# Tap rows as four products summed in PSUM, one shared exponential buffer and a new instruction order in an S4 convolution kernel

## The chip, the cores and the metric

The kernel runs on one core of a Trainium2 chip. The metric is the device time of one launch in microseconds (us), as the median of several runs. Some runs of a kernel take longer than the others: a run more than 1.5% above the fastest of the same kernel is called slow here, and all ratios use fast runs only. The granted clock is the share of full TensorE speed that the profile records; its mean does not tell slow from fast in this case (0.927 in the slow run of the changed kernel, 0.897 to 0.941 in its fast ones). Within a trace, TensorE is called warm where the granted clock is 1.00 and cold where it is 0.50. The traces have a span that starts at the first and ends at the last instruction; it is about 1.8 us shorter than the device time of the same run. Times "at" are us from the start of that span.

## The reference, cut to what matters

The output is a gated mix of a long convolution (S4) and a small routed feed-forward network. Only the first matters for the change.

```python
# L = 2048 steps, D = 512 channels, N = 128 modes
logdA = dt * (A_re + 1j * A_im)                      # D x N
P = jnp.exp(logdA[:, :, None] * l[None, None, :])    # l = 0 .. L-1
K = jnp.einsum("dn,dnl,dn->dl", Cc, P, dt * Bc).real # convolution kernel, D x L
y = irfft(rfft(u, 2 * L) * rfft(K, 2 * L))[:L] + u * Dskip
out = g * y + (1 - g) * routed_ffn(u)                # g: a sigmoid gate per step
```

The kernel does not compute all L exponentials of a mode. It writes a lag as a sum of an entry of a first table (32 lags) and an entry of a second (21 "slots"), makes both tables as exponential times sine or cosine, and lets TensorE contract their product over the modes. The transforms are matmuls with fixed matrices.

## The kernel before: the parts that matter

The channels are worked on in two halves of 256, h = 0 and 1. The rows of the second table (the "tap rows") hold 21 slots. Slots 0 to 8 come from exponentials and sines; slots 9 to 20 are complex products of earlier slots with two base values, made on VectorE. A complex product takes six operations: four multiplications, and two that combine.

```python
def cmul(h, outs, a, b, rda, rdb, wr):          # VectorE; index 0 imaginary, 1 real
    TT(q(0), a(0), b(0), MUL, ...)
    TT(q(1), a(1), b(0), MUL, ...)
    TT(outs(1), a(1), b(1), MUL, ...)
    TT(outs(0), a(0), b(1), MUL, ...)
    TT(outs(1), outs(1), q(0), SUB, ...)        # combine
    TT(outs(0), outs(0), q(1), ADD, ...)        # combine
# at the end of tab2(h):
cmul(h, ... slots 13 to 20 = slots 0 to 7 times base 1 ...)   # 128 x 2048 each
cmul(h, ... slots 9 to 12 = slots 5 to 8 times base 0 ...)    # 128 x 1024 each
```

The product of the two tables, `kgen`, follows on TensorE. I call it the tap-row product. It has 256 matmuls per half, each with 64 columns of weights and 42 moving columns. They add up in PSUM, TensorE's output memory; an eviction is the copy of a finished PSUM buffer by another engine:

```python
def kgen(h):
    for b0 in range(0, 64, 12):                  # 12 groups of 4 channels fill one PSUM buffer
        ...
        for g in range(b0, b0 + ng):
            for ct in range(2):
                for part in range(2):
                    hh.matmul(pb(64 * ct, 64, (g - b0) * 42, (1, 42)), TP[h][1 - part](...),
                              TQ[h][1 - part](0, 128, g * 84 + ct, (2, 42)),
                              start=(part == 0), stop=(part == 1), tile_position=(0, 64 * ct))
        EV(KA[h](...), pb(...), ...)             # eviction, on ScalarE or VectorE
    ...
```

After it come the spectrum of the convolution kernel (TensorE), the products of the spectra (VectorE, with some sums made by accumulating DMAs issued by GpSimd), the inverse transform (TensorE) and the output. Three more facts matter:

- The order of all some 620 operations is a fixed list `SEQ`; each engine works through its own part strictly in that order. A negative entry puts an operation that ScalarE or VectorE can do on VectorE.
- The 2 MB of inverse matrices, `G` (in the trace `c_inv`), are loaded to where first-table values of the second half lie, so their load starts when the last matmul of the second tap-row product is done.
- The input with the routed part added is read back from memory (`xp`, 2 MB, the "reload") for the output.

Of the kernel before, what the change touches and what calls it, by code (L numbers as in the profile page):

```python
# [9 lines left out]
BF = mybir.dt.bfloat16  # L10
# [48 lines left out]
class Prog:  # L59
# [48 lines left out]
    def schedule(self):  # L108
# [7 lines left out]
        for n in SEQ:  # L116
# [21 lines left out]
            if o.dma:  # L138
                t0 = st + (0.8 if e == POOL else c + 1.2)
                if o.nbytes > 20000:  # L140
                    t0 = max(t0, dma_free[e])
                took = o.nbytes / (150.0e3 if o.tag == "sum" else self.DMA_BW)
                if e != SP and dma_free[SP] > t0:
                    w = min(dma_free[SP] - t0, 7.0)
                    dma_free[SP] += took
                    if o.nbytes > 20000:
                        t0 += w
                    took *= 1.3
                if o.nbytes > 20000:
                    dma_free[e] = t0 + took  # L150
                o.end = t0 + took + 0.5 + o.late
            else:
                o.end = st + c + (0.13 if e == PE else 0.0)
# [130 lines left out]
def kspec_mats():  # L284
# [35 lines left out]
    "0 19 3 2 1 4 8 22 23 54 57 41 55 40 49 50 64 24 25 58 59 56 63 42 26 27 -179 -169 -167 -168 -180 -170 43 -177 39 37 5 -207 211 -178 170 -172 -174 180 "  # L320
    "-182 -184 184 17 172 -187 -189 182 -199 -188 68 9 210 -213 78 46 47 45 12 6 208 207 -210 213 66 217 65 84 -200 11 51 75 52 -190 10 29 28 30 31 32 103 "
    "185 48 36 91 77 53 18 20 21 61 -198 67 80 44 71 73 216 218 83 90 214 -216 38 86 72 60 107 62 15 112 -114 -115 -116 -121 121 14 223 222 16 122 123 85 "
    "174 175 76 70 13 219 220 124 125 126 127 144 128 -225 229 228 74 190 -194 -192 194 196 200 -204 -202 204 221 225 226 129 130 132 -132 133 134 135 192 "
    "195 256 258 259 136 7 -232 230 236 137 257 260 -262 263 138 139 140 202 -269 -266 -267 -268 205 141 142 162 145 34 227 233 232 -144 262 264 275 -317 "
    "276 274 269 -271 272 163 277 280 281 278 279 -314 282 283 164 271 273 284 285 -304 305 286 89 150 151 315 104 235 93 105 35 111 87 154 -156 79 33 152 "
    "156 98 237 242 241 362 96 -307 110 109 81 234 239 314 108 238 361 95 99 243 248 102 -305 287 289 -154 106 69 82 94 288 292 299 291 290 298 293 294 88 "
    "240 244 245 101 97 100 92 157 158 159 295 297 301 247 296 300 345 317 -321 318 319 -334 334 336 335 321 322 343 307 308 309 323 325 324 326 -311 311 "
    "312 337 -341 -339 341 346 349 -351 160 344 347 -349 327 -331 331 246 251 353 339 342 -381 -382 379 378 328 329 -372 -370 -371 -373 351 367 352 365 366 "
    "368 250 363 -253 354 355 357 -357 359 249 332 382 -384 385 373 374 375 389 388 376 -388 390 393 -392 394 384 254 358 253 364 377 386 392 395 398 397 "
    "399 396 400 402 401 405 406 404 412 403 407 409 411 408 413 255 410 414 360 419 420 415 421 452 416 451 453 417 418 423 422 455 427 431 432 424 425 "  # L330
    "454 456 428 429 430 433 434 146 147 -149 -150 161 165 435 436 426 437 438 116 117 118 119 439 441 -443 440 443 465 464 466 461 444 445 446 447 448 462 "
    "463 449 450 488 484 483 489 500 490 471 472 457 458 460 459 502 504 473 474 478 485 546 486 501 505 477 547 548 503 467 468 469 470 487 492 549 491 "
    "496 497 550 557 551 493 556 558 475 302 506 507 508 509 510 498 499 560 494 495 559 561 513 515 514 516 518 517 511 512 519 522 476 524 526 525 527 "
    "479 480 482 481 531 532 533 538 540 539 528 529 535 536 537 541 523 530 534 567 520 552 553 555 581 579 554 578 580 562 563 565 564 582 589 583 590 "
    "584 591 592 594 593 595 585 587 586 588 521 566 568 569 544 573 543 571 603 601 545 542 598 599 570 602 600 597 596 572 574 575 576 577 610 612 611 "
    "613 615 619 614 618 604 606 605 607 608 616 609 617 "
).split()]

KB = 1024


def bass_gated_mix__ssm_conv_s4__moe_arch_mod__prompt_kernel(nc, A_u, A_A_re, A_A_im, A_B_re, A_B_im, A_C_re, A_C_im, A_log_dt, A_Dskip,
# [22 lines left out]
    with ExitStack() as es:  # L365
# [63 lines left out]
        o_ = [190 * KB]  # L429
# [4 lines left out]
        CB = small("cb", 1792, BF); CF = small("cf", 640, F32); AL = small("al", 2048, F32); B16 = small("b16", 2048, F32)  # L434
        WW = small("ww", 2048, BF); SG = small("sg", 256, F32); SGB = small("sgb", 128, BF); RTS = small("rts", 1088, F32)
        OHT = small("oht", 64, BF); ZB = small("zb", 1024, BF); WL = small("wl", 16, BF); XS = small("xs", 16, BF)
        HB = small("hb", 448, BF); MSB = small("msb", 16, BF); DSK = small("dsk", 1024, BF); EB1 = small("eb1", NM * 512, BF); IDX = small("idx", 32, I32); HPI = small("hpi", 32, F32)
        assert o_[0] <= SBW, o_[0]
        oA, oB, oC, oD, oE, oF, oG, oI = [x * KB for x in (0, 16, 48, 64, 96, 117, 149, 170)]
# [16 lines left out]
        EB = [B("eb0", oG, NM * 512), EB1]  # L456
        XP = Buf(P, "xp", AR[:, :], "dram", 0, 4, BF)
        xp = nc.dram_tensor("xp", (L, D), BF).ap()
        QA = [B("qa%d" % i, o, 9 * KB) for i, o in enumerate((oG + NM * 512, oE))]
        BN = [(B("bni%d" % i, o, KB), B("bnr%d" % i, o + KB, KB)) for i, o in enumerate((oG + 14 * KB, oE + 9 * KB))]  # L460
        UN = B("un", oG + 16 * KB, 4 * KB)
# [3 lines left out]
        KA = [B("ka0", oG, 64 * 84), B("ka1", oE, 64 * 84)]  # L465
# [6 lines left out]
        SL = [B("sl%d" % i, o, 4 * KB) for i, o in enumerate([oI + 4 * KB * k for k in range(4)] + [oD + 26 * KB, oE + 11 * KB, oE + 15 * KB] + [oG + 4 * KB * k for k in range(1, 5)] + [oD + (6 + 4 * k) * KB for k in range(4)])]  # L472
        PR = [[(SL[4], SL[5], SL[6], SL[0]), tuple(SL[7:11])], [(SL[0], SL[1], SL[11], SL[12]), (SL[2], SL[3], SL[13], SL[14])]]
        YA = [B("ya%d" % i, o, 4 * KB) for i, o in enumerate((oI + 16 * KB, oE))]
# [81 lines left out]
        def two(buf, other, off, st):  # L556

            a, c = buf(0, 128, off, (st, 64), (1, 4)), other(0, 128, off, (st, 64), (1, 4))
            return bass.AP(a.tensor, a.offset, [a.ap[0], [c.offset - a.offset, 2], [st, 64], [1, 4]])
# [3 lines left out]
        def exps2(ts):  # L563
            for b in EB:
                P.op(POOL, lambda h, b=b: h.memset(b(0, 128, 0, (4 * NM, 64), (1, 4)), 1.0), [], [(b, ("e", 0))], cost=0.4)
            for i, m in enumerate(MAG2):
                if i:
                    AC(two(EB[0], EB[1], i * 4, 4 * NM), AL(0, 128, 0, (HC, 2), (4, 64), (1, 4)), ACTF.Exp, [AL], [(EB[0], ("e", i)), (EB[1], ("e", i))], scale=float(m), tset=ts)
# [48 lines left out]
        def tab2(h, ts):  # L617
            (qi, qr), (bi, br), eb = TQ[h], BN[h], EB[h]
# [19 lines left out]
            bn = lambda p, j, c: (bi, br)[p](0, 128, 4 * j, (8, 64), (0, c), (1, 4))  # L638
            cmul(h, lambda p: sl(p, 13, 8), lambda p: sl(p, 0, 8), lambda p: bn(p, 1, 8), ks, [bi, br], lambda p: [(tq(p), "n")])
            cmul(h, lambda p: sl(p, 9, 4), lambda p: sl(p, 5, 4), lambda p: bn(p, 0, 4), ks, [bi, br], lambda p: [(tq(p), "f")])  # L640
# [141 lines left out]
        def kgen(h):  # L782
            for b0 in range(0, 64, 12):
                ng = min(12, 64 - b0)
                pb = kgp[(b0 // 12) % 2]
                def mm(hh, b0=b0, ng=ng, pb=pb):
                    last = None
                    for g in range(b0, b0 + ng):
                        for ct in range(2):
                            for part in range(2):  # L790
                                last = hh.matmul(pb(64 * ct, 64, (g - b0) * 42, (1, 42)), TP[h][1 - part](0, 128, g * 128 + ct, (2, 64)),  # L791
                                                 TQ[h][1 - part](0, 128, g * 84 + ct, (2, 42)), start=(part == 0), stop=(part == 1), tile_position=(0, 64 * ct))
                    return last
                P.op(PE, mm, [*TP[h], *TQ[h]], [pb.buf], cost=ng * 4 * 0.03)
                EV(KA[h](0, 128, b0 * 42, (1, ng * 42)), pb(0, 128, 0, (1, ng * 42)), [pb.buf], [(KA[h], b0)])
# [82 lines left out]
        def inverse(h):  # L878
            for blk in (1, 0):
# [35 lines left out]
                for st in range(4):  # L915
                    tb = blk * 8 + st * 2
                    DMA([(dr(out, (1024 * blk + 256 * st) * D + h * HC, (2 * D, 128), (D, 2), (1, HC)), U(0, 128, tb * D + h * HC, (D, 2), (1, HC)))],
                        [(U, ("o", tb, h)), (U, ("o", tb + 1, h))], [], 131072, tag="final")
# [4 lines left out]
        exps2(2)  # L923
# [11 lines left out]
        DMA([(U(0, 128, j * 8 * D, (2 * D, 4), (1, 2 * D)), dr(xp, 1024 * j * D, (2 * D, 128), (256 * D, 4), (1, 2 * D))) for j in range(2)], [XP], [(U, t) for t in range(16)] + [(U, ("x", t)) for t in range(16)], 2097152)  # L935
        stage("tab1 1")
# [80 lines left out]
```

## Time and profile before

The median is 182.87 us (three runs, 182.21 to 183.17); the profiled run has a span of 180.8 us. The next lines are the activity by windows of the kernel before. Columns: the window, its length, and for each engine the busy time and in brackets the number of instructions; then the granted clock of TensorE, the DMA share and GB/s. PE is TensorE, PEld its weight loads, DVE is VectorE, ACT ScalarE, POOL GpSimd.

```profile
core 0: us, PE busy (x) PEld busy (x) DVE busy (x) ACT busy (x) POOL busy (x), PEclk, DMA share, GB/s
6.60:95.13 88.53, 71.27 (x778) 36.80 (x786) 80.39 (x148) 84.66 (x152) 0.71 (x2) 0.94 0.63 195
95.13:114.70 19.57, 11.32 (x82) 8.48 (x82) 19.30 (x21) 8.35 (x9) 0.00 (x0) 0.89 0.02 9
114.70:122.22 7.52, 6.83 (x256) 6.62 (x256) 6.55 (x11) 3.68 (x9) 2.83 (x3) 0.60 0.47 90
122.22:133.80 11.58, 7.32 (x82) 5.20 (x82) 10.78 (x12) 4.15 (x6) 2.24 (x3) 1.00 1.02 271
133.80:175.11 41.31, 40.76 (x352) 35.01 (x352) 36.02 (x47) 15.85 (x30) 11.18 (x10) 0.96 0.93 182
175.11:180.77 5.66, 0.00 (x1) 0.00 (x0) 0.88 (x2) 0.00 (x0) 0.00 (x0) 0.82 0.50 142
```

The first window ends with the last sine of the second half on ScalarE, the second with the end of the tap rows on VectorE (19.30 of 19.57 us busy), the third with the last matmul of the second tap-row product (256 matmuls), the fourth with the arrival of the inverse matrices, the fifth with the last matmul of the kernel. The first window is ScalarE's: the chain of waits runs over ScalarE for most of it. In the fifth both TensorE (40.76 of 41.31 us) and VectorE (36.02) are nearly full.

The groups of instructions by form, of before, show the operations that the change touches. Columns: line, engine, operation, names, shapes, count; busy us and mean ns of one; idle us before it and what ended the idle time.

```profile
L401 DVE TENSOR_TENSOR AR<-AR 128x2048 bf16<-128x2048 bf16 x52 | 62.0, 1219 | 4.2 <-DMA AR<-AR 3.0 <-PE ps L719 0.4 <-PE ps L791 0.4
...
L413 ACT ACTIVATE AR<-AR 128x256 bf16<-128x256 f32 x64 | 20.8, 403 | 1.9 <-DVE AR L401 1.9
...
L791 PE MATMUL ps<-AR 128*64 128x42 bf16 x512 | 11.6, 203 | 7.4 <-DVE AR L401 4.6 <-ACT AR L417 2.8
...
L583 ACT ACTIVATE AR<-AR 128x1024 int16<-128x1024 int16 x4 | 5.5, 1369 | 0.1
L413 ACT ACTIVATE AR<-AR 128x512 bf16<-128x512 f32 x9 | 5.3, 618 | 0.0
```

(Line numbers differ by a few from kernel to kernel; L400 and L401, or L416 and L417, are the same helper: L417 is the eviction from PSUM.) L401 is the helper of all VectorE operations with two inputs. L413 with 128x256 and 128x512 are the exponentials, L583 the absolute values that prepare a cosine, L791 the tap-row matmuls. Two lines from the list of waits of before (engine, line, what it waited for, us in total, times, longest):

```profile
PE ps L892 <- DMA AR<-c_inv: 3.3, 1, 3.3
...
DVE AR L401 <- DMA AR<-AR: 3.0, 2, 2.5
```

TensorE stands 3.3 us for the inverse matrices, and VectorE 3.0 us for accumulating DMAs.

### The profile page before, as it was taken

The numbers are of one execution on the slowest core, as the hardware profiler recorded it, in microseconds if no ns is written. First come the engines' busy times: TensorE is split into PE (matmuls) and PEld (weight loads), VectorE is DVE, ScalarE is ACT, GpSimd is POOL, SyncE is SP. The second block draws the span as 40 slices with busy tenths as digits, with TensorE's granted clock in tenths as the row PEclk, the third lists the DMA queues.
The fourth block names the chain that finished last, engine by engine and source line by source line (L and its number), as shares of the span: only waits on it lengthen the run. The fifth ranks groups of instructions, "written<-read, shape, count | busy, mean of one in ns | idle before, by whom it ended". The sixth has DMA issues, their size and how long they took to land.

```text
span 180.8 us, 3701 instructions
## 1 busy us (share of the span) xinstructions
PE 137.5 (76%) x1550; PEld 92.1 (51%) x1558; DVE 153.9 (85%) x240; ACT 118.6 (66%) x207; POOL 18.7 (10%) x26
## 2 busy tenths in 40 slices
PE   0039797996988999759946773689739999999970
PEld 0014263432555443444614552686528788888860
DVE  0377999899999998997879999989948999999570
ACT  2599999989999799999985272163501584425100
POOL 3000000000000000001000000053100125350500
PEclk9999996999996999987997999569987999999997
DMA  5999999595703950001621000079999659979995
GB/s 56 280 325 230 284 283 381 242 450 154 266 4 99 373 170 0 4 4 15 261 67 52 0 0 5 2 141 268 305 224 356 182 100 187 163 82 186 152 186 155
DMA packets 28338, 30.25 MB, mean 167 GB/s; under 512 B 13431, under 2 KB 22914, under 8 KB 28162
## 3 DMA queue, kind: packets, MB, share of 16 engines
q1 hardware_dynamic: 22626, 23.88, 42.6%
q0 software_dynamic: 4352, 5.77, 20.1%
q10 hardware_dynamic: 1344, 0.36, 1.8%
q8 instruction: 12, 0.20, 0.4%
q14 instruction: 4, 0.03, 0.1%
HBM read 19.26 MB, written 4.20 MB: 130 GB/s over the span
## 4 chain that ended last, share of the span: by engine, by line
ACT 33%; DVE 27%; PE 24%; DMA 10%; issue 3%; DVEq 0%; ACTq 0%
DVE AR L401 26%; ACT AR L413 14%; PE ps L892 10%; DMA AR<-AR 6%; ACT AR L587 6%; PE ps L743 5%; ACT AR L417 4%; PE ps L758 4%; DMA AR<-in_A_A_re_dram 3%; ACT AR L421 3%; ACT AR L583 2%; PE ps L761 2%; PE ps L895 1%; ACT L413 1%; PE ps L805 1%
## 5 line engine op out<-in xcount | busy, mean ns | idle before, releaser
L401 DVE TENSOR_TENSOR AR<-AR 128x1024 bf16<-128x1024 bf16 (+8 forms) x135 | 120.3, 931 | 13.8 <-DMA AR<-in_A_A_re_dram 6.7
L417 ACT ACTIVATE AR<-ps 128x1024 bf16<-128x1024 f32 (+3 forms) x41 | 34.2, 856 | 31.3 <-PE ps L827 20.1
L413 ACT ACTIVATE AR<-AR 128x256 bf16<-128x256 f32 (+5 forms) x91 | 40.4, 516 | 2.9 <-DVE AR L401 1.9
L743 PE MATMUL ps<-AR 128*128 128x512 bf16 x124 | 31.7, 410 | 13.2 <-DMA AR<-in_A_u_dram 11.8
L892 PE MATMUL ps<-AR 128*128 128x256 bf16 x256 | 33.9, 279 | 3.7 <-DMA AR<-c_inv 3.3
L892 PEld LDWEIGHTS ps<-AR 128*128 128x128 bf16 x256 | 25.3, 100 | 8.1 <-DVE AR L401 4.5
L743 PEld LDWEIGHTS ps<-AR 128*128 128x128 bf16 x128 | 13.1, 105 | 29.2 <-DMA AR<-in_A_u_dram 11.8
L827 PE MATMUL ps<-AR 128*128 128x256 bf16 x160 | 21.1, 291 | 6.9 <-ACT AR L417 6.9
L827 PEld LDWEIGHTS ps<-AR 128*128 128x128 bf16 x160 | 16.3, 105 | 11.5 <-ACT AR L417 8.6
L427 POOL DMA_DIRECT2D AR<-AR x14 | 14.8, 1194 | 68.0 <-DVE AR L401 56.9
L758 PE MATMUL ps<-AR 128*128 128x512 bf16 x60 | 16.3, 412 | 3.3 <-DVE AR L417 1.3
L791 PE MATMUL ps<-AR 128*64 128x42 bf16 x512 | 11.6, 203 | 7.4 <-DVE AR L401 4.6
L413 ACT ACTIVATE AR<-ps,AR 128x256 bf16<-128x256 f32 x24 | 10.1, 473 | 10.1 <-PE ps L895 7.7
L791 PEld LDWEIGHTS ps<-AR 128*64 128x64 bf16 x512 | 11.0, 132 | 9.2 <-DVE AR L401 4.9
L587 ACT ACTIVATE AR<-AR 128x1024 bf16<-128x1024 int16 (+1 forms) x14 | 14.5, 1052 | 0.6 <-DVE AR L401 0.3
L421 DVE TENSOR_SCALAR AR<-AR 128x256 int32<-128x256 f32 (+2 forms) x42 | 12.3, 333 | 0.9 <-ACT AR L587 0.9
L758 PEld LDWEIGHTS ps<-AR 128*128 128x128 bf16 x64 | 6.4, 105 | 10.5 <-issue 2.2
L417 DVE CAST AR<-ps 128x1024 bf16<-128x1024 f32 (+2 forms) x9 | 8.7, 979 | 1.7 <-PE ps L805 0.7
L945 POOL MEMSET AR<- 128x256 bf16 x2 | 0.7, 390 | 82.2 <-PE ps L791 82.2
L895 PE MATMUL ps<-AR 128*128 128x256 bf16 x32 | 8.7, 273 | 0.0
L421 ACT ACTIVATE AR<-AR 128x256 int32<-128x256 f32 x22 | 7.9, 407 | 0.2
L583 DVE TENSOR_SCALAR AR<-AR 128x1024 int32<-128x1024 int32 (+1 forms) x9 | 6.1, 673 | 2.1 <-ACT AR L413 2.1
(50 smaller groups left out, 85.6 us busy)
## 6 DMA issues: line engine op xcount, KB each, us to landing
AR<-AR POOLq DMA_DIRECT2D x8, 512.0 KB, 5.6
AR<-c_ksp SPq DMA_DIRECT2D x5, 512.0 KB, 3.9
AR<-c_fwd SPq DMA_DIRECT2D x4, 512.0 KB, 5.8
AR<-in_A_u_dram SPq DMA_DIRECT2D x2, 1024.0 KB, 8.1
AR<-c_inv SPq DMA_DIRECT2D x1, 2048.0 KB, 11.5
AR<-xp SPq DMA_DIRECT2D x2, 1024.0 KB, 12.1
out_dram<-AR SPq DMA_DIRECT2D x16, 128.0 KB, 3.4
AR<-in_B_w_up_dram SPq DMA_DIRECT2D x2, 896.0 KB, 8.4
```

The costliest lines, as they stand in the source:

```text
L401: return P.op(DVE, lambda h: h.tensor_tensor(out=o, in0=a, in1=b, op=op), rd, wr, cost=tt_cost(o, a, b), **k)
L413: return P.op(ACT, lambda h: h.activation(out=o, in_=a, func=func, scale=scale, bias=bias), rd, wr, cost=0.185 + nel(o) * 0.833e-3 + (0.09 ...
L417: return P.op((ACT, DVE), (lambda h: h.activation(out=o, in_=a, func=ACTF.Copy), lambda h: h.tensor_copy(o, a)), rd, wr, cost=(0.185 + n * ...
L421: return P.op((ACT, DVE), (lambda h: h.activation(out=o, in_=a, func=ACTF.Copy, scale=c), lambda h: h.tensor_scalar(out=o, in0=a, scalar1= ...
L427: P.op(POOL, lambda h: h.dma_start(o, i, accum_op=ALU.add), rd, wr, cost=1.4, nbytes=nbytes, dma=True, tag="sum")
L587: return x.activation(out=so(2), in_=lo, func=ACTF.Sin, scale=-SC16 if m else SC16, bias=HPI(0, 128, 0, (1, 1)) if m else 0.0)
L743: last = h.matmul(o, F[ft](0, 128, ((par * 4 + st) * 2 + part) * 128, (1, 128)), U(0, 128, (blk * 8 + st * 2 + par) * D, (1, D)), start=(i ...
L758: last = h.matmul(o, F[ft](0, 128, ((4 + st) * 2 + part) * 128, (1, 128)), UN(0, 128, st * D, (1, D)), start=False, stop=(st == 3 and blk ...
L791: last = hh.matmul(pb(64 * ct, 64, (g - b0) * 42, (1, 42)), TP[h][1 - part](0, 128, g * 128 + ct, (2, 64)), TQ[h][1 - part](0, 128, g * 84 ...
L827: last = hh.matmul(pb(0, 128, n * 256, (1, 256)), KPU[u](0, 128, tau * 128, (1, 128)), KC[h](0, 128, jg * 256, (1, 256)), start=(k == 0), ...
L892: last = hh.matmul(pb(0, 128, e * 256, (1, 256)), G(0, 128, ((par * 2 + part) * 4 + ft) * 512 + (2 * t2 + e) * 128, (1, 128)), X(0, 128, h ...
L895: last = hh.matmul(pb(0, 128, e * 256, (1, HC)), CB(0, 128, 768, (1, 128)), U(0, 128, (blk * 8 + (2 * t2 + e) * 2 + par) * D + h * HC, (1, ...
```

## The change

The intent is to relieve VectorE: the combining of slots 9 to 20 moves into PSUM. The four products are all kept, two of them in new buffers `EX`, and each tap-row matmul gets a partner of 24 columns with the same weights, which adds the second pair of products to the same PSUM columns. That makes 512 matmuls per half. One exponential buffer now serves both halves in turn, so nine exponentials of 128x512 become eighteen of 128x256. Every second output transfer of the last half is issued by ScalarE. Buffers have moved, and `SEQ` is new throughout: among others, four more absolute values stand on ScalarE, and the reload now stands ahead of the inverse matrices.

```diff
-            cmul(h, ... slots 13 to 20 ...)
-            cmul(h, ... slots 9 to 12 ...)
+            SCL(nb(...), bi(...), -1.0, [bi], [nb])
+            for j, s, c, m in ((13, 0, 8, 1), (9, 5, 4, 0)):
+                TT(sl(1, j, c), sl(1, s, c), bv(br), MUL, ...)
+                TT(sl(0, j, c), sl(0, s, c), bv(br), MUL, ...)
+                TT(xv(1), sl(0, s, c), bv(nb), MUL, ...)      # xv: into EX[h]
+                TT(xv(0), sl(1, s, c), bv(bi), MUL, ...)
...
-   last = hh.matmul(pb(64 * ct, 64, (g - b0) * 42, (1, 42)), TP.., TQ.. (2, 42), start=(part == 0), stop=(part == 1), ...)
+   last = hh.matmul(pb(64 * ct, 64, (g - b0) * 42, (1, 42)), TP.., TQ.. (2, 42), start=(part == 0), stop=False, ...)
+   last = hh.matmul(pb(64 * ct, 64, (g - b0) * 42 + 18, (1, 24)), TP.., EX.. (2, 24), start=False, stop=(part == 1), ...)
...
-        EB = [B("eb0", oG, NM * 512), EB1]
+        EB = [EB1, EB1]
...
-   ... 131072, tag="final")
+   ... 131072, tag="final", eng=ACT if h == 1 and st % 2 else SP)
...
(SEQ: all lines replaced; buffer addresses and the slots of the product buffers: cut)
```

## The prediction

> **What bounds the kernel now.** The activity by windows shows three stages. Until 95.2 us ScalarE is the limit: 84.7 us busy of the 88.6 us from 6.6 to 95.2, and the chain of waits runs almost wholly over ScalarE. From 95.2 to 114.0 VectorE is (18.6 of 18.8 us): the complex products of the second half's tap rows, released by the last sine. Then the second half's kernel generation on TensorE runs to 122.2, at a granted clock of 0.59; its end releases the 2 MB load of the inverse matrices, for which TensorE idles 3.3 us (list of waits) until 133.9. From there TensorE (40.8 of 41.2 us busy) and VectorE are both nearly full until 175.1, then 5.7 us of output.
>
> **What the change does, per half, by the groups by form.**
> - VectorE loses two combining operations of 128x2048 (1.22 us each) and two of 128x1024 (0.69): about 3.5 us net of overlap; it gains one small negation (0.3 us, for one half on ScalarE).
> - TensorE: each of 256 42-column matmuls gets a 24-column partner with the same weights loaded again. Before, warm, 96 took 1.71 us (18 ns each). I estimate 28 to 35 ns for a pair: +2.5 to 4.5 us per half.
> - ScalarE: 9 exponentials of 128x512 (0.62 us) become 18 of 128x256 (0.40; about 0.31 back to back): +0.8 us.
> - The new order moves work between engines. Before the last sine, four more absolute values stand on ScalarE (1.36 us there, 0.69 on VectorE), six fewer angle scalings (0.33 each), one fewer eviction. I count +3 us of ScalarE before the last sine. VectorE takes two kernel-spectrum evictions (1.2 us each) of the product stage.
> - Reload of U now stands before the inverse matrices on the queue and its scatter is issued earlier. The Trainium skill (DMA: Bandwidth & Descriptors, "Issuing engines are not separate DMA queues") says that all queues share the same 16 engines; in this trace the inverse matrices took 11.7 us while accumulations ran beside them. Now all overlap more.
> - Half of the last output issues move to ScalarE's queue: some tenths.
>
> **On the critical path.** The first half's saving falls in the stage that ScalarE bounds: worth little. The last sine moves from 95.1 to about 97 (95.5 to 98.5). The second half's saving is fully on the path: from the last sine to the end of the tap rows 15.4 us instead of 18.8, so that ends near 112.5 instead of 114.0. Kernel generation then takes 11 to 12 us instead of 8.2 and eats this; the inverse matrices are issued 1 to 2 us later and land 1 to 4 us later. After them TensorE has 41 us of work with about 1 us of slack.
>
> **Prediction.** 183.5 us, 179.5 to 187.0 in 8 of 10. Faster by over 2%: 0.15; within 2%: 0.68; slower by over 2%: 0.17.
>
> **What would show it.** Last sine at 96 to 98.5 us; second half's tap rows 15 to 16 us long after it; second half's kernel generation 11 to 12 us; TensorE waiting 3 to 5 us for the inverse matrices, which land at 134.5 to 138; from there about 40 us to the last matmul.
>
> **What would make it wrong.** Faster: weights of the second matmul hidden wholly (28 ns a pair); ScalarE without gaps; inverse matrices landing within 9 us because accumulations no longer collide with them. Slower: reload and matrices sharing bandwidth so that both are late; accumulations landing after their products.

## More of the kernel before

The page's list of DMA queues has a queue of its own for instructions (packets, MB, share of the DMA engines):

```profile
q8 instruction: 12, 0.20, 0.4%
```

## The result, and the profile after

The changed kernel takes 189.59 us in the median of four runs (188.88 to 193.0, of which the 193.0 is slow); the kernel before, on the same chip, takes 183.02 us (four runs, 182.21 to 183.65). The ratio of the fast runs is 1.0349, with a 95% interval of 1.029 to 1.0408: slower. A ratio here is the mean time of one kernel's fast runs over that of the other's of the same rounds, so it is not quite the ratio of the medians that I quote. The result is right.

The same windows in the changed kernel (same columns; cut at the same steps):

```profile
6.60:100.68 94.08, 80.18 (x1064) 44.73 (x1064) 80.78 (x152) 88.36 (x160) 0.56 (x2) 0.93 0.60 187
100.68:116.40 15.72, 10.77 (x60) 7.22 (x60) 15.55 (x17) 7.79 (x12) 0.00 (x0) 0.67 0.01 2
116.40:131.64 15.24, 9.26 (x512) 8.79 (x512) 8.83 (x10) 1.85 (x4) 7.46 (x3) 1.00 0.53 108
131.64:142.62 10.98, 7.33 (x82) 5.40 (x82) 10.04 (x13) 4.15 (x6) 0.85 (x1) 0.83 0.83 334
142.62:182.78 40.16, 40.12 (x352) 35.09 (x352) 36.94 (x47) 14.64 (x29) 12.05 (x11) 0.96 0.89 148
182.78:187.77 4.99, 0.00 (x1) 0.00 (x0) 0.88 (x2) 0.00 (x0) 0.00 (x0) 0.90 0.64 184
```

The two columns of windows give the account of the 7.0 us between the two spans (187.77 and 180.77):

| step | before | after | difference |
|---|---|---|---|
| last sine, at | 95.13 | 100.68 | +5.55 |
| from there to the end of the tap rows | 19.57 | 15.72 | -3.85 |
| second tap-row product | 7.52 | 15.24 | +7.72 |
| load of the inverse matrices | 11.58 | 10.98 | -0.60 |
| from their arrival to the last matmul | 41.31 | 40.16 | -1.15 |
| output | 5.66 | 4.99 | -0.67 |

VectorE's saving is there and as large as it was meant to be. More than that is lost in two places: before it, by a later last sine, and after it, by a tap-row product that takes twice as long although the clock granted to it rose from 0.60 to 1.00, and although TensorE is busy in only 9.26 of its 15.24 us. The groups of the changed kernel that answer to those shown above:

```profile
L401 DVE TENSOR_TENSOR AR<-AR 128x2048 bf16<-128x2048 bf16 x48 | 57.2, 1218 | 4.8 <-DMA AR<-AR 3.3 <-PE ps L725 1.1
...
L413 ACT ACTIVATE AR<-AR 128x256 bf16<-128x256 f32 x82 | 25.9, 403 | 2.0 <-DVE AR L401 2.0
L797 PE MATMUL ps<-AR 128*64 128x42 bf16 x512 | 19.2, 192 | 3.1 <-ACT AR L417 1.6 <-DVE AR L401 1.0 <-DVE AR L417 0.5
L799 PE MATMUL ps<-AR 128*64 128x24 bf16 x512 | 19.2, 183 | 5.4 <-issue 5.4
...
L584 ACT ACTIVATE AR<-AR 128x1024 int16<-128x1024 int16 x7 | 9.6, 1366 | 0.2
```

VectorE has four operations of 128x2048 fewer (52 to 48). The 512 extra matmuls of 24 columns (L799) have 5.4 us of idle time before them, which ended with "issue": the profile shows nothing that TensorE waited for. The same in the list of waits, where the wait for the inverse matrices is 2.6 us, and VectorE's for accumulating DMAs has grown to 7.1:

```profile
DVE AR L401 <- DMA AR<-AR: 7.1, 2, 3.8
...
PE ps L799 <- issue: 5.4, 3, 4.0
...
PE ps L900 <- DMA AR<-c_inv: 2.6, 1, 2.6
```

The timeline of TensorE in the second tap-row product, only those lines where idle time ended with "issue" (start, length, engine, line, names, shapes; in square brackets the idle time before):

```profile
121.58 0.20 PE L799 MATMUL ps<-AR 128*64 128x24 bf16 x1 [0.98 <-issue]
...
125.04 0.20 PE L799 MATMUL ps<-AR 128*64 128x24 bf16 x1 [0.50 <-issue]
...
131.24 0.20 PE L799 MATMUL ps<-AR 128*64 128x24 bf16 x1 [3.97 <-issue]
```

And the instruction queue of the changed kernel:

```profile
q8 instruction: 16, 0.26, 0.6%
```

The queue makes 16 transfers instead of 12, 0.26 MB in all, so about 16 KB each. That fits the Trainium skill, "Runtime: NRT & Kernel Launch", section "Instruction fetch mechanics", which says that the instruction memory is a FIFO refilled in blocks of 16 KiB, 256 instructions, over a queue of its own. A matmul is two instructions, a weight load and the matmul, so 512 matmuls are four blocks where 256 were two. In the records of that queue (in the packed trace; the views of the profile do not list them one by one) the transfers within the second tap-row product ended at 120.14, 123.67 and 129.85 us. TensorE resumed after its gaps at 121.58, 125.04 and 131.24, each time 1.4 us after a transfer. While it runs warm, the starts of its matmuls are 16 ns apart, so 256 instructions last 2.05 us, while the three transfers ended 3.5 and 6.2 us apart. The page says that the cost of crossing a block boundary is mostly hidden; here it is not. That is theory A: TensorE runs out of instructions.

The other traces agree. In the six with the doubled second product of 42 and 24 columns (after, e3, e4, e5, e6, e8), thirteen gaps of 0.46 to 3.97 us ended with "issue" 1.2 to 1.6 us after a transfer of that queue had ended; one more, of 0.48 us in e6, did not.

### The profile page after: what moved, and what is told of

It is laid out like the page before. It is cut to its first block, busy times and chain, and to the rows that moved or that the text cites. A ratio compares the mean times of both kernels' runs of the same rounds, so it can differ in the third digit from the quotient of the medians.

```text
span 187.8 us, 4736 instructions
## 1 busy us (share of the span) xinstructions
PE 147.7 (79%) x2070; PEld 101.2 (54%) x2070; DVE 153.0 (81%) x239; ACT 118.7 (63%) x211; POOL 22.4 (12%) x25
## 4 chain that ended last, share of the span: by engine, by line
PE 40%; ACT 21%; DVE 20%; DMA 10%; issue 4%; SPq 2%; DVEq 0%; ACTq 0%
PE ps L900 15%; DVE AR L401 15%; PE ps L749 9%; DMA AR<-c_inv 6%; ACT AR L588 6%; ACT AR L413 5%; DMA AR<-c_fwd 5%; ACT AR L584 4%; PE ps L764 4%; PE ps L835 4%; ACT AR L421 2%; ACT AR L417 2%; DVE AR L417 2%; DVE AR L421 2%; PE ps L903 2%
## 5 line engine op out<-in xcount | busy, mean ns | idle before, releaser
L401 DVE TENSOR_TENSOR AR<-AR 128x1024 bf16<-128x1024 bf16 (+8 forms) x127 | 113.3, 930 | 21.0 <-DMA AR<-AR 7.1
L417 ACT ACTIVATE AR<-ps 128x1024 bf16<-128x1024 f32 (+3 forms) x33 | 28.4, 879 | 38.0 <-PE ps L835 19.0
L749 PE MATMUL ps<-AR 128*128 128x512 bf16 x128 | 32.7, 411 | 13.2 <-DMA AR<-c_fwd 12.6
L900 PE MATMUL ps<-AR 128*128 128x256 bf16 x256 | 33.3, 277 | 2.6 <-DMA AR<-c_inv 2.6
L835 PE MATMUL ps<-AR 128*128 128x256 bf16 x160 | 23.4, 311 | 7.3 <-ACT AR L417 6.3
L799 PE MATMUL ps<-AR 128*64 128x24 bf16 x512 | 19.2, 183 | 5.4 <-issue 5.4
L797 PE MATMUL ps<-AR 128*64 128x42 bf16 x512 | 19.2, 192 | 3.1 <-ACT AR L417 1.6
L799 PEld LDWEIGHTS ps<-AR 128*64 128x64 bf16 x512 | 18.5, 118 | 5.7 <-issue 5.7
L797 PEld LDWEIGHTS ps<-AR 128*64 128x64 bf16 x512 | 18.4, 117 | 4.4 <-ACT AR L417 1.7
L427 POOL DMA_DIRECT2D AR<-AR x14 | 15.2, 1268 | 39.9 <-DVE AR L401 31.1
L764 PE MATMUL ps<-AR 128*128 128x512 bf16 x64 | 17.3, 411 | 1.6 <-DVE AR L417 1.5
L417 DVE CAST AR<-ps 128x1024 bf16<-128x1024 f32 (+3 forms) x17 | 15.8, 943 | 1.5 <-PE ps L749 0.9
L421 DVE TENSOR_SCALAR AR<-AR 128x256 int32<-128x256 f32 (+3 forms) x49 | 13.7, 324 | 2.3 <-ACT AR L588 2.3
L584 ACT ACTIVATE AR<-AR 128x1024 int16<-128x1024 int16 (+1 forms) x9 | 11.7, 1302 | 0.3
```

The lines of the kernel that those rows point to most:

```text
L401: return P.op(DVE, lambda h: h.tensor_tensor(out=o, in0=a, in1=b, op=op), rd, wr, cost=tt_cost(o, a, b), **k)
L417: return P.op((ACT, DVE), (lambda h: h.activation(out=o, in_=a, func=ACTF.Copy), lambda h: h.tensor_copy(o, a)), rd, wr, cost=(0.185 + n * ...
L421: return P.op((ACT, DVE), (lambda h: h.activation(out=o, in_=a, func=ACTF.Copy, scale=c), lambda h: h.tensor_scalar(out=o, in0=a, scalar1= ...
L584: q = P.op((ACT, DVE), (lambda x: x.activation(out=lo, in_=lo, func=ACTF.Abs), lambda x: x.tensor_scalar(out=w, in0=w, scalar1=16384.0, sc ...
L749: last = h.matmul(o, F[ft](0, 128, ((par * 4 + st) * 2 + part) * 128, (1, 128)), U(0, 128, (blk * 8 + st * 2 + par) * D, (1, D)), start=(i ...
L764: last = h.matmul(o, F[ft](0, 128, ((4 + st) * 2 + part) * 128, (1, 128)), UN(0, 128, st * D, (1, D)), start=False, stop=(st == 3 and blk ...
```

## The experiments

All kernels ran beside the kernel before on the same chip; its median there was 183.68 us (with e1 to e4), 183.48 us (e5, e6, e7, b1) or 182.06 us (e8, e10, e11, b2; this set ran on another chip). The kernels of the tables are the runs of this section; "order" tells whose `SEQ` they follow. The times are medians of all runs, slow ones included (two of five in e1, one of four in b1); the ratios use fast runs alone. For e8 and e11 the intervals exclude 1, but whether the difference reaches 2% is unclear.

| run | order | tap rows, first / second half | time us | ratio (95%) |
|---|---|---|---|---|
| after | new | new / new | 189.59 | 1.0349 (1.029-1.0408) |
| e1 | old | old / old, matmuls split | 189.5 | 1.0312 (1.0243-1.038) |
| e2 | new | new / new, one matmul of 66 columns | 192.09 | 1.0489 (1.0434-1.0543) |
| e3 | new, reload late | new / new | 192.52, mostly slow | none |
| e4 | new, absolute values on VectorE | new / new | 194.3 | 1.0611 (1.0549-1.0673) |
| e5 | new, reload late, two sums on VectorE | new / new | 190.39 | 1.0366 (1.0309-1.0422) |
| e6 | old | new / new | 188.68 | 1.0284 (1.0234-1.0335) |
| e7 | new | old / old | 196.11 | 1.0688 (1.0642-1.0733) |
| e8 | old | old / new | 185.72 | 1.0181 (1.013-1.0232) |
| e10 | new, reload late | old / old | 192.96 | 1.0609 (1.0537-1.0681) |
| e11 | old | new / new, one matmul of 66 columns | 179.37 | 0.9844 (0.9792-0.9896) |
| b1 | old, matrices loaded early | old / old | 184.47 | 1.0026 (0.9964-1.0088) |
| b2 | old, outputs on two queues | old / old | 181.97 | 0.998 (0.9936-1.0023) |

The stages in the profiled runs, in us, as in the account above:

| run | last sine at | tap rows | first product | second product | matrices | to last matmul | output | span |
|---|---|---|---|---|---|---|---|---|
| before | 95.13 | 19.56 | 10.51 | 7.46 | 11.54 | 41.33 | 5.66 | 180.77 |
| after | 100.68 | 15.71 | 13.10 | 15.18 | 10.95 | 40.17 | 4.99 | 187.77 |
| e1 (slow) | 95.94 | 19.56 | 11.01 | 15.03 | 9.05 | 45.07 | 5.70 | 190.44 |
| e2 | 98.95 | 15.72 | 13.11 | 9.81 | 16.82 | 42.81 | 5.32 | 189.52 |
| e6 | 101.41 | 15.72 | 15.28 | 13.55 | 8.94 | 42.74 | 4.92 | 187.37 |
| e7 | 100.02 | 19.20 | 11.08 | 9.69 | 16.45 | 43.02 | 5.29 | 193.77 |
| e8 | 98.10 | 15.71 | 10.50 | 13.48 | 10.94 | 41.38 | 4.91 | 184.60 |
| e10 | 100.33 | 19.19 | 11.06 | 9.70 | 10.00 | 47.08 | 5.19 | 191.58 |
| e11 | 97.18 | 15.71 | 10.26 | 7.47 | 10.66 | 41.45 | 4.91 | 177.48 |

### e1: the old kernel with the second product's matmuls split

The columns stay, the instructions of the second half double.

```diff
-   hh.matmul(.., (1, 42)), .., TQ.. (2, 42), ..)
+   for c0 in (0, 21) if h else (0,):
+       hh.matmul(.. + c0, (1, 21)), .., TQ.. + 2 * c0 (2, 21), ..)     # half 1
```

> The kernel before, with each 42-column tap matmul of the second half cut into two of 21 columns on the same weights: the columns are the same, TensorE's instructions of that stage double; the result stays right. Theory A (TensorE runs out of instructions: its instruction blocks of 16 KB come by DMA and a stage of very short matmuls eats a block in about 2 us): the second kernel generation grows from 8.2 us to 12 to 16 us with gaps whose cause the profile calls issue, and the time from 183 to 187 to 190 us. Rival B (the added columns cost): columns are unchanged, so at most 1 us. Rival C (the earlier reload slows the stage): no reload moves here, so at most 1 us of gaps.

The time is 189.5 us, ratio 1.0312. This edit alone, in the old kernel, costs nearly as much as the whole change. Its profiled run fell in the slow state, so I read only the stage from it, and rest on the fast timed runs; how the stage went in those is not traced. TensorE's timeline in the second product, its three longest pieces:

```profile
115.56 7.64 PE L793 MATMUL ps<-AR 128*64 128x21 bf16 x278 [5.07 <-DVE AR L401]
...
123.38 6.36 PE L793 MATMUL ps<-AR 128*64 128x21 bf16 x224 [0.18 <-issue]
...
130.14 0.45 PE L793 MATMUL ps<-AR 128*64 128x21 bf16 x10 [0.40 <-issue]
```

The stage takes 15.03 us instead of 7.46. It ran cold, at a granted clock of 0.50, and had hardly a gap: 32 matmuls every 0.85 us, 27 ns each, whether 42 columns wide (the old kernel, cold, also 27 ns) or 21. So a cold matmul of this size costs by the instruction, not by the column. That the columns cost (rival B) is refuted: they are unchanged, and the fast runs are 3.1% slower. But the gaps that theory A expected came to only 0.6 us; here the price was that of the cold matmuls themselves.

### e2: the changed kernel with one matmul of 66 columns for each pair, in the second half

```diff
+   if h:
+       hh.matmul(pb(64 * ct, 64, (g - b0) * 38, (1, 66)), TP.., TQ.. (2, 66), start=(part == 0), stop=(part == 1), ..)
+       continue
```

Half the instructions, the same columns; the sums of this half are wrong. The comparison with the reference passed nevertheless, so it is no proof of correctness here.

> The kernel after, with the 42-column and the 24-column matmul of the second half replaced by one of 66 columns: same columns, half the instructions; wrong results on purpose. Theory A: the second kernel generation falls from 15.3 us to 8 to 10 us without issue gaps, time from 189.6 to 182.5 to 184.5 us. Rival B (columns): stays above 13 us, time above 188. Rival C (reload): gaps of 3 us or more stay, time above 187.

```profile
114.72 2.93 PE L798 MATMUL ps<-AR 128*64 128x66 bf16 x144 [2.59 <-DVE AR L401]
...
121.23 3.30 PE L798 MATMUL ps<-AR 128*64 128x66 bf16 x112 [3.58 <-DVE AR L417]
```

For the stage theory A holds: no gap is ended by "issue", and the second product takes 9.81 us, of which 3.58 are a wait for an eviction that stood behind other work on VectorE. For the time it missed: 192.09 us, slower still. The list of DMA issues of this kernel (names, engine, count, KB, us from issue to landing) shows where it went:

```profile
AR<-xp SPq DMA_DIRECT2D x2, 1024.0 KB, 12.5
AR<-c_inv SPq DMA_DIRECT2D x1, 2048.0 KB, 16.8
```

The matrices were issued 7.1 us earlier than in the changed kernel, at 124.57 instead of 131.66, while the reload was still running, and took 16.8 us. The Trainium skill, "DMA: Bandwidth & Descriptors", section "Issuing engines are not separate DMA queues", says that all transfers end up on the same 16 engines and interleave; this pair agrees. In the changed kernel the long tap-row product had softened this conflict: when its matrices were issued, 0.55 of the reload's 2.1 MB had moved. In e2 nothing of it had, and all of it went beside the matrices, with 0.65 MB of accumulating DMAs.

### e3: the changed kernel with the reload behind the matrices

```diff
-SEQ: ... 461 462 298 474 ...                (298: the reload)
+SEQ: ... 461 462 474 ... 485 298 ...        (485: the inverse matrices)
```

> The kernel after with the reload of U moved behind the inverse matrices on its queue, as in the kernel before; the scatter stays early. Theory A in its strict form (number of instructions alone): the gaps stay, the stage stays at 15 us, time 189 to 190. Rival C (the instruction blocks wait behind the reload's packets): the 4.0 us gap falls under 1 us, the stage to about 11.5 us, time 185 to 187 us.

Three of its four runs and the profiled one are slow, so there is no ratio; the fast one took 189.21 us. In the slow profile "issue" gaps of 1.54 and 3.75 us are still there. The fast traces of e6 and e8, below, say the same: their reload is issued 0.4 us behind the matrices, after the product, and gaps of up to 1.37 and 2.06 us ended with "issue" all the same. So rival C, which puts the gaps down to the reload, falls. The matrices now land in 7.6 us:

```profile
AR<-c_inv SPq DMA_DIRECT2D x1, 2048.0 KB, 7.6
```

The reload, however, lands at 151.25 instead of 137.74, and the stretch to the last matmul grows by more than was won (slow profile; e5, which is fast, has the same late reload, a load of 7.94 us and a stretch of 44.28 us).

### e4: four absolute values back on VectorE

```diff
-SEQ: ... 200 ... 260 ... 388 ... 396 ...
+SEQ: ... -201 ... -261 ... -389 ... -397 ...
```

> The kernel after with four absolute values put back from ScalarE (1.36 us each) to VectorE (0.69), at the same places of the order. If the later last sine (100.7 us instead of 95.1) comes from ScalarE's load, it moves to 95.5 to 97.5 us and the time falls by 3 to 5 us, to 184.5 to 186.5. If it comes from the waits of the new order instead, the last sine stays above 99 and the time above 188.

The last sine came later, at 105.04 us, and the time rose to 194.3 us. Both lie where the second branch of my expectation put them, but that does not show this branch, since the edit made new waits of its own. ScalarE's busy time up to then did fall, but it now waited for VectorE (list of waits, up to 106 us; L583 is the absolute value on VectorE):

```profile
ACT AR L587 <- DVE AR L583: 8.7, 3, 3.8
```

VectorE works in order too, and in this order it reaches the absolute values late. Moving a cost between engines without re-ordering tells little.

### e5: reload late, and the first accumulating DMAs replaced by VectorE sums

```diff
-SUMS = ((0, 0), (0, 1), (1, 0), (1, 1))
+SUMS = ((0, 1), (1, 0), (1, 1))            (and the SEQ of e3)
```

> The kernel after, reload behind the inverse matrices and the first pair of sums added on VectorE (2.4 us more there) instead of by accumulating DMAs: beside the scatter, almost no data DMA runs in the second kernel generation. If the instruction blocks are late because data DMAs fill the engines, the gap of 3.8 to 4.0 us that after, e3 and e4 all had falls under 1.5 us and the stage to 10 to 12.5 us. If the fetch is slow by itself, the stage stays at 14 to 16 us and a gap of over 3 us stays.

TensorE's waits around the second product:

```profile
PE ps L796 <- DVE AR L416: 2.6, 1, 2.6
...
PE ps L798 <- issue: 0.5, 1, 0.5
```

The gap of about 4 us at the end of the product is gone, and 0.5 us of "issue" is left. This does not show that the instruction block came sooner: the last two transfers of the stage ended at 123.14 and 128.85 us, 5.7 us apart against 6.2 in the changed kernel. TensorE stood 2.6 us for an eviction on VectorE and ran cold in part, at 27 ns (granted clock 0.77 in the stage), so it needed the block later. The product took 14.73 us and the time did not fall (190.39 us).

The queue records of the six traces say more. After each of the thirteen gaps named above, take the time from TensorE's restart to the start of the next block's transfer. Six times the DMA engines were nearly idle in that time (share of 0.13 or less), and the transfer started 1.0 to 1.1 us after the restart. Seven times they were full (share of 0.87 or more), with accumulating DMAs or with the loads, and it started 1.7 to 5.0 us after. So in these traces the blocks are late where the engines are full of data (e3's is a slow profile); this is read from traces, and no run was made to test it alone.

### e6 and e7: the change's two parts apart

e6 has the arithmetic, the buffers, the split exponentials and the two output queues of the change in the order of before, on before's engines. e7 has the new order and buffers with the old six operations and 256 matmuls per half. For both the new `SEQ` was made by mapping the operations one to one.

```diff
 e6 (against after)
-SEQ = (the new order)
+SEQ = (before's order and engines; the second half's nine exponentials put in as one block further on)
 e7 (against after)
-            SCL(nb ...); four products into TQ and EX
+            cmul(h, ... slots 13 to 20 ...); cmul(h, ... slots 9 to 12 ...)
-   hh.matmul(.., (1, 42)) ; hh.matmul(.., (1, 24))
+   hh.matmul(.., (1, 42))
```

> The change's four products, shared exponentials and buffers, in the order and on the engines of the kernel before. If the later last sine comes from the new order and its division of work, it returns to 94 to 96.5 us; tap rows end near 111, the second kernel generation still takes 13 to 16 us, time 184 to 187.5. If it comes from the shared exponentials or the buffers, the last sine stays above 99 and the time above 188.

> The kernel after with the old six-operation products and single tap matmuls, in the new order. The last sine stays near 100 to 102 us, tap rows take 18 to 19 us again, the second kernel generation 8 to 9 us; time 185 to 188. If the order alone were harmless, 183 to 184.

e6 takes 188.68 us, almost all of the loss. Its last sine was expected at 94 to 96.5 us, or above 99 if the exponentials or buffers were to blame; it came at 101.41. The timeline of ScalarE shows a reason that neither branch had:

```profile
85.26 1.15 ACT L587 ACTIVATE AR<-AR 128x1024 bf16<-128x1024 int16 x1
90.35 1.71 ACT L416 ACTIVATE AR<-ps 128x504 bf16<-128x504 f32 x3 [3.94 <-PE ps L798]
```

ScalarE stood 3.94 us for an eviction of the first tap-row product, which now takes 15.28 us instead of 10.51, with the sines of the second half in line behind it (e8 tells how much of the delay this is). VectorE pays in the same way in the second half (list of waits from 100 us on):

```profile
DVE AR L416 <- PE ps L798: 5.8, 1, 5.8
```

It stands 5.8 us in order behind the last eviction of the second product. In before that wait is 0.5 us. So the doubled matmuls do not only delay TensorE: each engine that evicts them loses the time too.

e7 was expected at 185 to 188 us and took 196.11: the new order is much worse for the old arithmetic than for the new. So the losses of the two parts, 2.8% and 6.9%, do not add up to that of the change, 3.5%. Its last sine is late as well (100.02), without any doubled matmul. Its matrices again shared the DMA engines with the reload:

```profile
AR<-xp SPq DMA_DIRECT2D x2, 1024.0 KB, 12.1
AR<-c_inv SPq DMA_DIRECT2D x1, 2048.0 KB, 16.4
```

### b1: before, with the inverse matrices loaded early

```diff
-        G = B("g", oF + 16 * KB, 16 * KB)
+        G = B("g", oI, 16 * KB)            # over the sine buffers; product buffers take its old place
```

> The kernel before with the inverse matrices in the place of the sine buffers, free after the last sine, instead of the second half's first table, free only after the second kernel generation: they load from about 101 us on an idle DMA. TensorE's 3.3 us wait for them goes, sums land in 5 to 7 us instead of 10 to 12; time 179.5 to 182. If VectorE's sums bound the stage anyway, 182 to 183.5.

The matrices land at 107.75 us and TensorE never waits for them, yet the time is 184.47 us, ratio 1.0026: the same. The last matmul ends at 175.44 us, as in before (175.11). So in before the wait of 3.3 us for the matrices is worth nothing that these runs can show. The chain of waits of b1 runs, after the second product, over VectorE and over an accumulating DMA of 11.69 us, as that of before does (11.73 us). A gain in the tail has to move VectorE as well as TensorE.

### e8: the new arithmetic in the second half only, in the old order

```diff
-            (four products, EX and doubled matmuls for both halves, as in e6)
+            if h == 0:  (cmul and 256 matmuls, as before)
+            else:       (four products and 512 matmuls)
```

> The order of before, with the changed buffers and the shared exponentials, but four products and doubled matmuls in the second half only; the first half has the old six operations and 256 matmuls. Theory S (in the old order the last sine came late, 101.4 us with the new arithmetic in both halves, because ScalarE stood 3.9 us in order behind evictions of the doubled first tap-row product): first tap-row product 10 to 11.5 us, ScalarE's wait behind it under 1 us, last sine at 95.5 to 97.5 us. Rival T (the shared exponential buffer and the new layout delay the sines): last sine after 100 us although the first product is short. Both: tap rows of the second half about 3 us shorter than before's 18.8, second tap-row product 13 to 15.5 us, VectorE waits over 3 us for its last eviction, time 183 to 187 us.

The time is 185.72 us. The first product is back at 10.50 us, ScalarE's wait behind it is gone, and the last sine comes at 98.10 us instead of 101.41. So the doubled first product accounts for 3.3 of the 6.3 us by which e6's sine was late. Theory S expected the sine at 97.5 us at the latest, so part of T is right too: 3.0 us remain. Of these, ScalarE's busy time explains 0.7 us (87.48 to 88.21 us up to the last sine), which is the split exponentials. The largest new wait is this one on ScalarE's timeline:

```profile
32.52 1.28 ACT L221 ACT_TABLE_LOAD   x1 [2.07 <-DVE AR L400]
```

At the end of a block of exponentials ScalarE stands 2.07 us for VectorE, in order, before it loads its other table; before does not have this wait. The second product took 13.48 us, and VectorE stood 5.5 us behind its last eviction, as expected.

### e10: e7 with the reload behind the matrices

```diff
-SEQ of e7: the reload ahead of the inverse matrices
+SEQ of e10: the reload right behind them
```

> The old six operations and single matmuls in the new order, as in the run with 196.1 us, but with the 2 MB reload issued behind the inverse matrices. Theory: the reload beside the matrices made them land 16.4 us after issue; behind them they land 7 to 11 us after issue, at 136 to 140 us, and the time is 186 to 191 us. Rival (the new order's other moves, above all the later sums, hold the end back): matrices land early, but the time stays at 193 to 197 us.

```profile
AR<-c_inv SPq DMA_DIRECT2D x1, 2048.0 KB, 10.0
```

The matrices land after 10.0 instead of 16.4 us, but the stretch to the last matmul grows from 43.0 to 47.1 us, and the time is 192.96 us, 0.8% better in the ratio, with intervals that overlap. The theory was right for the transfer; for the time its rival comes nearer, just at its edge. From the changed kernel to e5 the late reload goes with a stretch that is 4.1 us longer too (e5 also adds two sums to VectorE). What else in the new order holds the end back with the old arithmetic I did not take further apart.

### e11: one matmul of 66 columns for each pair, in the old order

```diff
-   (42 columns from TQ, then 24 columns from EX, as in e6)
+   hh.matmul(pb(64 * ct, 64, (g - b0) * 40, (1, 66)), TP.., TQ.. (2, 66), start=(part == 0), stop=(part == 1), ..)
```

All columns of the change, half its matmul instructions, sums wrong in both halves (the comparison shows a relative error of 2.2%).

> The order of before, four products in both halves, but each pair of tap-row matmuls (42 and 24 columns) replaced by one of 66 columns: the same columns, half the instructions, sums wrong on purpose. Theory A (the price of the change is the number of matmul instructions): first product 10 to 12 us, second 7.5 to 10 us, last sine at 96 to 98 us, tap rows of the second half done by 111 to 114 us, time 179 to 182.5 us, so the four products would pay but for the instructions. Rival B (VectorE's later sums and products set the end in any case, as with the early matrices): stages as under A, time 182.5 to 185 us. Rival C (columns cost): products 14 us or more, time over 186 us.

The time is 179.37 us, ratio 0.9844: below before (whether by 2% is unclear), in the range of theory A. TensorE's timeline in the second product:

```profile
112.94 3.47 PE L796 MATMUL ps<-AR 128*64 128x66 bf16 x192 [0.32 <-DVE AR L400]
116.82 0.98 PE L796 MATMUL ps<-AR 128*64 128x66 bf16 x48 [0.41 <-ACT AR L416]
119.96 0.45 PE L796 MATMUL ps<-AR 128*64 128x66 bf16 x16 [2.16 <-ACT AR L416]
```

192 matmuls of 66 columns run in 3.47 us, 18 ns each, and the stage takes 7.47 us, as in before with 42 columns (there cold in most of the stage and almost without a wait, here warm with 2.6 us of waits for evictions on ScalarE). Against e6, which differs in nothing but the number and width of these matmuls (1.0284), the halved instructions are worth 0.044 of the time, about 8 us (each against its own runs of before, on two chips). Weight loads and matmuls are halved together, so which of the two counts is not separated. Rival C, that columns cost, falls once more, and so does B, that VectorE's tail would swallow the gain: the stretch to the last matmul is 41.45 us, as in before, and simply starts earlier.

This is not a version to use, because the 24 columns are not added to the other 42. A right kernel of this shape would evict 66 columns for each group instead of 42. Three evictions of 504 columns took 1.42 us back to back on ScalarE in before, so I estimate 1.4 us more of evictions per half ((66 - 42) x 64 columns at 0.94 ns), and more matmuls to add the parts, which I did not work out. That is as much as the 2.7 us that e11 wins.

### b2: before, with the outputs on two queues

```diff
-   ... 131072, tag="final")
+   ... 131072, tag="final", eng=ACT if h == 1 and st % 2 else SP)
```

> Before, with every second output transfer of the second half issued by ScalarE's queue, as in the change, and nothing else. If that part of the change is worth what the two traces differ by, the stretch from the last matmul to the end goes from 5.7 to about 5.0 us and the time is 0.3 to 0.9 us below before: ratio 0.995 to 0.999. Rival: the output tail is bound by the transfers, and stays at 5.7 us; ratio 1.0.

The output stretch went from 5.66 to 4.66 us in the trace; the ratio is 0.998, and its interval includes 1. The effect in the trace is real but too small to be told in the time.

## Why the prediction was wrong

1. **"Kernel generation then takes 11 to 12 us instead of 8.2": the step that failed.** It took 15.2. (The boundary that the prediction used before was one short VectorE operation too early; the stage itself takes 7.5 us.) The estimate for a pair of matmuls, 28 to 35 ns, was right: 32 ns warm. Wrong was the sum. It assumed that TensorE is always fed. It was not: for 5.4 us of the stage it had no instruction to run, and each gap ended 1.4 us after a transfer of the instruction queue (trace of after; e2 and e11, with half the instructions, have no such gap there). Without these gaps the stage would have taken about 9.7 us by my estimate (15.18 less 5.45), less than the prediction said. And where the stage runs cold, as in e1, a matmul costs 27 ns each however narrow it is, so that doubling them doubles the stage.

2. **"The last sine moves from 95.1 to about 97": too little.** It came at 100.7. ScalarE's busy time up to it rose from 84.66 to 88.36 us (windows), 3.7 us, near the "+3 us" that the prediction itself had counted and then halved. Four more of the large absolute values (L583 before: 4 of 128x1024; L584 after: 7, and two instead of one of 128x768) are 5.3 us of it, the split exponentials about 0.8, and fewer evictions and angle scalings take some of it back. The other 1.85 us are idle time, for which the prediction had no term. This account is read from the traces and not shown by an edit, since e4 made new waits. e7 does show that the new order with its engines, buffers and split exponentials brings 4.9 us without any doubled matmul. In the old order the sine is as late (6.3 us in e6) by another way: 3.3 us of it come through the eviction of the doubled first product (e8).

3. **"The second half's saving is fully on the path", 15.4 us for the tap rows: right.** They took 15.7 us, in every run with the new arithmetic, against 19.2 to 19.6 with the old.

4. **Inverse matrices "1 to 4 us later": wrong by inheritance.** They were issued 9.4 us later, because their issue waits for the second product, and landed 8.8 us later. The load itself took 10.95 us against 11.54. The prediction's fear that reload and matrices share the bandwidth came true in part: 1.5 MB of the reload moved beside the matrices in the changed kernel, but in before 1.0 MB of accumulating DMAs did, so the load was no longer. With the whole reload beside them it was (e2 and e7, 16.8 and 16.4 us).

5. **"About 40 us to the last matmul" and the output tenths: right.** 40.2 us and 0.67 us less. TensorE's wait for the matrices was 2.6 us rather than 3 to 5. VectorE's wait for accumulating DMAs grew to 7.1 us, one of the prediction's fears, and yet the stretch is not longer.

So the sum failed in two terms. The second tap-row product grew by 7.7 us where the prediction had it grow by 3 to 4, and the last sine moved by 5.5 us where it had about 2. The smaller terms (matrices, tail, output) gave back 2.4 us. The probability of "slower" was set at 0.17. Both terms were taken as if each engine's work could be added up without asking what feeds it and what stands in order behind it.

What stays open: a test by itself of the delay of the instruction blocks by other DMAs, whether weight loads or matmuls are the ones to count, which part of the late last sine an edit could take back, and which moves of the new order cost the old arithmetic its 6% (e10).

## What to carry to other kernels

Moving a VectorE operation into PSUM by a second, narrow matmul trades elements for instructions; before counting columns, count matmul instructions, and check in the trace whether gaps that end with "issue" follow the transfers of the instruction queue. Widening a matmul was free here (66 columns cost as much as 42), doubling their number was not. And where engines work in order, price the wait of the engine that evicts as well as that of the engine that multiplies.

## What the Trainium skill lacked or had wrong

- "Runtime: NRT & Kernel Launch", "Instruction fetch mechanics": the blocks of 256 instructions and their own queue are confirmed (16 transfers, 0.26 MB), but fetching was not "mostly hidden". Short warm matmuls used up 256 instructions in 2.05 us, the transfers of blocks ended 3.5 and 6.2 us apart, and TensorE stood 5.4 us in one stage, resuming 1.4 us after each block.
- "TensorE: Matmul & The Clock Gate", "Wait — 56ns, not 53.3ns?": it says that starts of matmuls never come closer than about 25 ns. Here, with weights of 64 columns put alternately on two halves of the array, the starts were 16 ns apart warm (24 and 42 columns in turn), and 18 ns for 192 matmuls of 66 columns. The runs do not test weights over the whole array, so the figure fails only as worded, without an exception for this use.
- The same page: it gives no measured figure for matmuls this narrow while the clock is low. The runs show 27 ns each at a granted clock of 0.50, for 21 columns as for 42.
- "DMA: Bandwidth & Descriptors", "Issuing engines are not separate DMA queues": confirmed; the section gives no size for it. The 2 MB of matrices took 7.8 us in b1, issued long before the reload, 10.95 in the changed kernel with 1.5 MB of the reload beside them, and 16.4 to 16.8 us in e7 and e2 with all of the reload and some 0.65 MB of accumulating DMAs.
